# Two repeated waits ahead of the last matmul of each half of the up products, on one core

## The chip, the cores and the metric

The kernel runs on one core of one Trainium2 chip. The metric is the device time of one execution in microseconds, and the number to predict is the median of several executions. The core has five engines with an instruction stream each: TensorE (PE, with its weight loads shown apart as PEld), VectorE (DVE), ScalarE (ACT), GpSimd (POOL) and SyncE (SP). [...]

## What is computed

Two branches read the same 2048 x 512 input and a sigmoid gate per row mixes them:

```python
def reference(A_x, A_wq, A_wk, A_wv, A_wo, A_beta, B_x, B_w_gate, B_w_up, B_w_down, gate_w):
    x = A_x
    g = _sigmoid((x * gate_w).sum(-1, keepdims=True))
    a = _A_ref(x, A_wq, A_wk, A_wv, A_wo, A_beta)      # attention in 4 segments, 32 heads of 16
    b = _B_ref(x, B_w_gate, B_w_up, B_w_down)          # (gelu(x wg) * (x wu)) wd, inner width 1792
    return g * a + (1 - g) * b
```

The attention works on four segments of 512 rows. Inside a segment each head has causal softmax attention; across segments it reads a running memory M (16 x 16 per head) and its normaliser z, and both are updated with the segment's keys and values. A sigmoid of beta mixes the two per head.

## The kernel before

**Work and tiles.** Everything is done per segment s = 0 to 3. `project` (L504) makes K, Q and V with 128x128 weights and 512 moving columns; `memory` (L567) reads and updates M and z; `attend` (L683) computes scores for all heads in fills of the 2048-column PSUM tile psX (`fill`, L633: matmuls at L645, exponentials on ACT at L661, the causal mask on POOL at L667) and then the products with V (L698), turned and normalised on DVE (L557, L709, L710); `glu_gate` and `glu_up` (L800, L818) make 14 gate and 14 up products per segment; `outputs` (L827) makes four row blocks with the down weights (L837) and the attention's output weights (L854), joins them on DVE (L858) and stores them by DMA (L863).

**The up products.** `dense` (L483) builds one product of four accumulating matmuls as two tasks of two matmuls each: U3_5a and U3_5b are the first and second half of the up product of tile 5 in segment 3. There are 4 x 14 = 56 up products, so 112 such tasks. All dense products share line L487, and a 512-column PSUM bank (psD) of four takes each of them.

**Order and waits.** The order of all tasks is one long list, `ORDER` (L1015), found by a planner that is not part of the kernel. A word names a task, and behind the colon the PSUM bank or buffer that it begins, or the engine that it runs on (a for ACT, d for DVE) where an eviction may run on either. `Emitter.plan` (L176) derives what each instruction depends on, `finalize` (L205) turns that into waits on counting semaphores and leaves out every wait that an earlier one of the same engine has already covered, and `emit` (L237) writes the waits (L241) ahead of the instruction.

**The two paths and the last branch.** The kernel holds a fast program, and behind it a general one that is only run when the fast one's softmax sums are out of range. A flag is computed on the chip (L728 to L738), every engine loads it into a register (L742), and then its fast stream ends with a compare-and-branch (L961) over the general program to a label `done`. The general program is long: on TensorE the fast stream has 2767 entries (a matmul entry becomes a weight load and a matmul) and the general one 3801. Early in each stream stands a hint (L951) that names that branch as one likely to be taken; `HINT` (L27) says behind how many entries (6 on TensorE).

```python
        em.emit(eng, slice(p.start, p.start + HINT[eng]))
        ahead = e.mark_branch_hint_location()
...
        e.br_eq(regs[eng], GOOD, on_true=done, on_false=general).branch_hint(ahead)
        with nc.body(general, valid_engines=[e.engine]):
            em.emit(eng, q)
...
        nc.switch_bb(done)
```

At the end all engines meet in a barrier (the lines at L971), which SyncE joins once the last output has landed (L992).

Of the kernel before, what the change touches and what calls it, by code (L numbers as in the profile page):

```python
# [160 lines left out]
class Emitter:  # L161


    def __init__(self, nc, engmap):
        self.engmap = engmap
        self.cnt = {e: nc.alloc_semaphore(f"cnt_{e}") for e in (PE, ACT, DVE, POOL)}
        self.dma_val = {}
        self.res = {}
        self.streams = {e: [] for e in ENGINES}
        self.order = []  # L170

# [65 lines left out]
    def emit(self, eng, part):  # L237
        e = self.engmap[eng]
        for spec in self.streams[eng][part]:
            for sem, val in spec.waits:  # L240
                e.wait_ge(sem, val)  # L241
            ins = spec.fn(e)
# [11 lines left out]
def _build(es, nc, A_x, A_wq, A_wk, A_wv, A_wo, A_beta, B_w_gate, B_w_up, B_w_down, gate_w, out):  # L254
# [30 lines left out]
    ident = sb("ident", [P, P])  # L285
# [14 lines left out]
    gr1 = sb("gr1", [P, 16], F32)  # L300
# [639 lines left out]
    for turn_ in (order, program(True)[0].in_turn()):  # L940
# [4 lines left out]
        parts.append({e: slice(began[e], len(em.streams[e])) for e in ENGINES})  # L945
    em.finalize()
# [74 lines left out]
V0_0a:0 Qev0_1:a V0_3a:1 st0_0A:0 V0_1a:2 V0_0b exp0_0A vones0 causal Vev0_0:d V0_1b V0_3b V0_2a:3 Vev0_1:d Vev0_3:d
ld_wg1 st0_0B:0 V0_2b exp0_0B phka0_2 Vev0_2:a vsh0_00 phkc0_0 G0_6a:2 vsh0_01 G0_6b msk0_0A Gev0_6:d G0_2a:0 G0_1a:1
st0_0C:0 G0_1b G0_3a:3 Gev0_1:d exp0_0C G0_0a:2 G0_0b G0_2b Gev0_0:d st0_0D:0 vsh0_20 exp0_0D vsh0_21 msk0_0B G0_3b
betab Gev0_3:d ld_wu1 Q1_3a:2 ld_wo00 msk0_0D Q1_3b G1_6a:1 G1_6b Qev1_3:d Gev0_2:d bexp ld_wo10 Gev1_6:d st0_0E:0
Q1_2a:3 K1_1a:2 V1_3a:0 Q1_2b K1_1b exp0_0E Qev1_2:d msk0_0C st0_1A:0 V1_0a:1 msk0_0E V1_0b V1_3b Kev1_1:a Vev1_0:d gq
pv0_0:23 exp0_1A phkb0_2 ld_wo30 Vev1_3:d st0_1B:0 exp0_1B V1_1a:1 Q1_1a:0 V1_1b Q1_1b tp0_d01:1 Qev1_1:a K1_2a:3
phkc0_2 ld_x2_1 st0_1C:0 Vev1_1:d G0_4a:1 exp0_1C G0_4b tp0_d00:2 K1_0a:2 K1_0b K1_3a:0 Gev0_4:d Kev1_0:a st0_1D:0
exp0_1D ktr0_1 kpada1_1 G0_5a:1 pvp0_00 G1_1a:2 G0_5b K1_3b pvp0_01 Gev0_5:a K1_2b st0_2A:0 ld_wo11 ktr0_3 exp0_2A
G1_1b G1_7a:1 ktr0_2 Kev1_3:d Kev1_2:d G0_10a:0 ld_x2_2 Gev1_1:d G1_7b G0_8a:3 msk0_1A gph G0_10b gd0_10 kpada1_0
G0_8b ld_wo01 G1_13a:2 gd1_7 G1_13b msk0_1D msk0_1C G0_9a:0 kpada1_2 phqa1_2 gd1_13 G0_9b ld_wu0 G0_13a:1 G0_13b  # L1030
G0_7a:2 gd0_8 msk0_1B gd0_9 ot0_0 pv0_1:03 gd0_13 st0_2B:0 G1_9a:1 gelu0 G0_7b tp0_d10:1 G1_9b G0_12a:0 gd0_7
tp0_d11:0 G1_8a:3 G0_12b G0_11a:2 pvp0_10 G1_8b pvp0_11 gd1_9 G0_11b gd0_12 Q1_0a:1 kpadb1_1 gd1_8 Q1_0b U0_3a:3
Qev1_0:d gd0_11 U0_3b G1_5a:0 G1_5b ktr0_0 ld_wd0 h0_3 ld_wo21 phka1_0 kpada1_3 U0_9a:1 U0_11a:3 U0_11b exp0_2B U0_9b
st0_2C:0 ot0_1 mz0:2 phkb1_0 msk0_2B h0_9 U0_5a:1 h0_11 ld_x2_0 exp0_2C U0_5b msk0_2C phka1_2 ld_gw U0_8a:3 Gev1_5:a
ld_xg0 gs0 st0_2D:0 kpadb1_2 U0_8b exp0_2D mzacc0 U0_6a:2 U0_6b h0_5 U0_1a:0 h0_8 U0_4a:3 ld_xg1 gs1 h0_6 st0_2E:0
msk0_2A U0_1b U0_4b U0_7a:2 phkc1_0 h0_1 exp0_2E U0_13a:1 U0_7b st0_3A:0 ld_xg2 ld_xg3 h0_4 G1_0a:0 phkb1_2 G1_0b
ld_xg4 msk0_2D U0_13b h0_7 gs2 exp0_3A msk0_2E ld_xg5 pv0_2:32 Gev1_0:a h0_13 st0_3B:0 U0_0a:0 tp0_d20:1 U0_10a:1
V1_2a:3 V1_2b U0_10b exp0_3B gs3 tp0_d21:0 phqa1_0 st0_3C:0 U0_2a:2 h0_10 U0_0b gs4 msk0_3A h0_0 U0_2b h0_2 G1_2a:1
kpadb1_0 Vev1_2:a G1_2b exp0_3C ld_x2_3 kpadb1_3 st0_3D:0 msk0_3B G1_3a:0 mzm0 K2_1a:2 ld_xg6 K2_1b G1_4a:3 exp0_3D
msk0_3C msk0_3D Gev1_2:d Kev2_1:a G1_3b st1_0A:0 U0_12a:1 exp1_0A ld_xg7 pvp0_21 G1_4b Gev1_3:d gs5 U0_12b pvp0_20  # L1040
h0_12 pv0_3:20 zq0 st1_0B:0 phqb1_2 out0_1_0:1 out0_1_1 ld_wd1 exp1_0B tp0_d30:2 phkc1_2 K2_3a:2 ld_x3_3 tp0_d31:0 gs6
out0_1_2 gs7 ktr1_0 st1_0D:0 K2_3b Q2_3a:0 ktr1_2 vsh1_00 out0_1_3 Gev1_4:a Kev2_3:d exp1_0D Q2_3b gz0 K2_2a:3 msk1_0B
ot0_2 ktr1_1 Qev2_3:a st1_0E:0 gr0 vsh1_01 phqc1_2 V2_3a:2 K2_0a:0 V2_3b K2_2b Vev2_3:d pvp0_30 exp1_0E out0_1_4
st1_0C:0 K2_0b go0 Kev2_2:a ld_wo20 ktr1_3 phqb1_0 Kev2_0:d out0_3_0:3 vsh1_21 msk1_0A G1_11a:2 pvp0_31 out0_0_0:0
ot0_3 out0_0_1 out0_0_2 wev0_1:d exp1_0C out0_0_3 out0_0_4 wo0_1_0:1 vsh1_20 out0_3_1 G1_11b wev0_0:d out0_3_2
# [81 lines left out]
```

## Time and profile before

| what | value |
|---|---|
| median of 3 runs | 267.12 us (267.05, 267.12, 267.35) |
| profiled execution, its own time | 268.07 us |
| its span, first to last instruction | 266.3 us |
| mean granted TensorE clock | 0.997 |
| TensorE matmuls busy | 254.0 us, 95% of the span |
| DVE, ACT, POOL busy | 214.5, 209.6, 96.6 us |
| last arithmetic (the copy of the flag, L738) ends | 261.0 us |

The span leaves 1.8 us of the profiled execution's own time outside, and that execution took 0.95 us longer than the median. Engines named with a q (PEldq, SPq) are their sequencers: waits, branches and DMA issues, which are not counted as busy. A group's "idle before" is time in which its engine stood still just ahead of it, with what ended that. DMA queues are named by number; those of the kind "instruction" bring the engines' own code.

### The profile page before, as it was taken

The page shows a single profiled execution, that of the slowest core. Times are in us where ns is not written, and L with a number is a line of the kernel's source. Part 1 is how long each engine was busy: PE and PEld are TensorE (multiplying, and loading weights), DVE is VectorE, ACT ScalarE, POOL GpSimd, SP SyncE. Part 2 cuts the span into 40 slices and gives each one's busy share as a digit, 9 for nine tenths or more (in the row PEclk, how much of TensorE's full clock was granted, in tenths as well). Part 3 has the DMA queues.
Part 4 walks back from the last instruction along what each step waited for, and adds up shares of the span by engine and source line. Part 5 has one row for each costly group of instructions (what it writes and reads, how often), then busy time and mean ns, then how long its engine had stood idle before and what let it go on. Part 6 is the DMA issues. An engine that isn't in the chain of part 4 may idle for free.

```text
span 266.3 us, 6561 instructions
## 1 busy us (share of the span) xinstructions
PE 254.0 (95%) x2729; PEld 112.4 (42%) x2766; DVE 214.5 (81%) x421; ACT 209.6 (79%) x174; POOL 96.6 (36%) x159
## 2 busy tenths in 40 slices
PE   7999999999999999999999999999999999999991
PEld 4634434444344444444434344334444443434450
DVE  0676776689999797999798989998988986959872
ACT  2578999989899999999988879568889976577420
POOL 6024332065551526160452644433407217263400
PEclk9999999999999999999999999999999999999998
DMA  6897179802547203002021001000110000000011
GB/s 205 237 177 234 39 108 192 245 23 62 158 62 100 61 20 109 12 0 63 0 64 42 20 2 62 2 21 2 43 35 7 0 2 21 21 22 1 22 39 47
DMA packets 26624, 17.19 MB, mean 65 GB/s; under 512 B 14302, under 2 KB 26078, under 8 KB 26590
## 3 DMA queue, kind: packets, MB, share of 16 engines
q1 hardware_dynamic: 26014, 16.27, 25.3%
q10 hardware_dynamic: 576, 0.46, 0.6%
q8 instruction: 22, 0.36, 0.6%
q14 instruction: 12, 0.10, 0.1%
HBM read 10.36 MB, written 2.10 MB: 47 GB/s over the span
## 4 chain that ended last, share of the span: by engine, by line
PE 93%; issue 2%; DMA 2%; DVE 1%; SPq 0%
PE psD L487 51%; PE psD L837 18%; PE psX L645 9%; PE psD L698 6%; PE psD L854 5%; DMA pt<-in_A_x_dram 2%; PE psD L582 1%; PE psD L515 1%; PE psX L600 0%; PE psD L509 0%; DVE ost L858 0%; SPq L357 0%; PE psD L588 0%; PE psX L908 0%; DVE kD L526 0%
## 5 line engine op out<-in xcount | busy, mean ns | idle before, releaser
L661 ACT ACTIVATE pt<-psX 128x2048 bf16<-128x2048 f32 x72 | 135.1, 1877 | 28.6 <-PE psX L645 27.4
L667 POOL TENSOR_TENSOR pt<-pt,ctri 128x256 bf16<-128x256 bf16 x128 | 91.2, 719 | 151.8 <-ACT pt L661 147.3
L487 PE MATMUL psD<-xT,wu 128*128 128x512 bf16 x214 | 54.1, 380 | 1.4 <-issue 1.3
L837 PE MATMUL psD<-wd,gb 128*128 128x512 bf16 x217 | 54.1, 380 | 0.9 <-issue 0.8
L487 PE MATMUL psD<-xT,wg 128*128 128x512 bf16 x217 | 54.1, 380 | 0.9 <-issue 0.8
L824 DVE TENSOR_TENSOR gb<-psD,gb 128x512 bf16<-128x512 f32 x56 | 37.3, 684 | 8.6 <-PE psD L487 8.3
L837 PEld LDWEIGHTS psD<-wd,gb 128*128 128x128 bf16 x224 | 20.5, 98 | 26.1 <-issue 2.8
L487 PEld LDWEIGHTS psD<-xT,wu 128*128 128x128 bf16 x224 | 20.3, 98 | 26.1 <-issue 2.8
L487 PEld LDWEIGHTS psD<-xT,wg 128*128 128x128 bf16 x224 | 20.1, 98 | 26.4 <-issue 3.2
L557 DVE STREAM_TRANSPOSE tT<-psD 128x512 f32<-128x512 f32 x35 | 24.1, 703 | 7.7 <-PE psD L698 5.8
L645 PE MATMUL psX<-qT,kD 32*128 32x192 bf16 (+7 forms) x512 | 28.5, 287 | 0.0
L645 PEld LDWEIGHTS psX<-qT,kD 32*128 32x128 bf16 x512 | 8.2, 92 | 25.2 <-ACT pt L661 20.9
L698 PE MATMUL psD<-pt,vnat 64*17 64x128 bf16 (+7 forms) x512 | 18.8, 283 | 0.0
L698 PE MATMUL psD<-pt,vsh 64*17 64x128 bf16 (+7 forms) x512 | 18.3, 283 | 0.0
L710 DVE SCALAR_TENSOR_TENSOR ob<-tT,gq,rcall 128x256 bf16<-128x256 f32 x32 | 16.6, 517 | 1.1
L487 PE MATMUL psD<-wv,xT 128*128 128x512 bf16 x61 | 16.8, 380 | 0.4 <-issue 0.3
L487 PE MATMUL psD<-xT,wq 128*128 128x512 bf16 x59 | 16.2, 379 | 0.7 <-issue 0.5
L480 DVE CAST gb<-psD 128x512 bf16<-128x512 f32 x19 | 12.9, 686 | 3.9 <-PE psD L487 3.9
L854 PE MATMUL psD<-wo,oT 128*128 128x512 bf16 (+1 forms) x69 | 15.5, 354 | 0.5 <-issue 0.5
L698 PEld LDWEIGHTS psD<-pt,vnat 64*17 64x17 bf16 x512 | 11.6, 86 | 8.9 <-POOL pt L667 4.2
L815 ACT ACTIVATE gb<-psD 128x512 bf16<-128x512 f32 x28 | 14.8, 603 | 0.6 <-PE psD L487 0.5
L842 ACT ACTIVATE wds<-psD,omgt 128x512 f32<-128x512 f32 x8 | 5.5, 686 | 12.1 <-PE psD L837 7.4
(99 smaller groups left out, 275.8 us busy)
## 6 DMA issues: line engine op xcount, KB each, us to landing
xg<-in_A_x_dram SPq DMA_DIRECT2D x16, 128.0 KB, 2.2
out_dram<-ost SPq DMA_DIRECT2D x15, 128.0 KB, 1.7
wg<-in_B_w_gate_dram SPq DMA_DIRECT2D x2, 896.0 KB, 6.8
wu<-in_B_w_up_dram SPq DMA_DIRECT2D x2, 896.0 KB, 5.9
wd<-in_B_w_down_dram SPq DMA_DIRECT2D x2, 896.0 KB, 6.7
vsh<-vnat SPq DMA_DIRECT2D x16, 68.0 KB, 2.1
wq<-in_A_wq_dram SPq DMA_DIRECT2D x2, 256.0 KB, 5.3
wv<-in_A_wv_dram SPq DMA_DIRECT2D x1, 512.0 KB, 3.9
```

The costliest lines, as they stand in the source:

```text
L480: (DVE, 0.60, [I(lambda e: e.tensor_copy(dst, src()), [bk(sl), *reads], writes)]),
L487: one(f"{name}{'abcd'[h // 2]}", PE, 2 * T_MM, [I(lambda e, i=i: e.matmul(BK[sl.i][:, :], lhs(i), rhs(i), start=(i == 0), stop=(i == n - 1 ...
L557: one(f"tp{name}", DVE, 0.605, [I(lambda e, ts=ts, bank=bank: e.transpose(tT[ts.i][:, :], bank()), [key], [("tT", ts)])])
L645: ins.append(I(lambda e, c=c, kb=kb, ncol=ncol, c0=c0, g=g: e.matmul(XALL[:, g * 512 + c0:g * 512 + c0 + ncol], kD[b][quad(g), c, kb, :], ...
L661: one(f"exp{s}_{name}", ACT, 2048 * 0.000833 + 0.05, [I(lambda e: e.activation(pt[slot][:, :, :], xin, ACTF.Exp, scale=ATT_SCALE), [("X", ...
L667: ins.append(I(lambda e, mv=mv: e.tensor_tensor(mv, mv, cm, ALU.mult), [("pt", slot), ("causal",)], [("pt", slot)]))
L698: ins.append(I(lambda e, kb=kb, slot=slot, c0=c0, n=n, g=g, c=c, r0=r0, sl=banks[j], va=va: e.matmul(BK[sl.i][32 * c:32 * c + 17, 64 * kb: ...
L710: I(lambda e, ts=ts, t=t, j=j, dst=dst, r=r: e.scalar_tensor_tensor(out=dst, in0=t_rows(ts, 16), scalar=gq[:, 2 * t + j:2 * t + j + 1], in ...
L815: one(f"gd{s}_{ft}", ACT, 0.485, [I(lambda e, gi=gi, f=f, sl=sl: e.activation(gb[gi][:, f, :], BK[sl.i][:, :], ACTF.Gelu_apprx_tanh), [bk( ...
L824: one(f"h{s}_{ft}", DVE, 0.605, [I(lambda e, sl=sl, gi=gi, f=f: e.tensor_tensor(gb[gi][:, f, :], BK[sl.i][:, :], gb[gi][:, f, :], ALU.mult ...
L837: mm.append(I(lambda e, fb=fb, gi=gi, f=f, q=q, sl=sl: e.matmul(BK[sl.i][:, :], gb[gi][:, f, q], wd[:, fb, :], start=(fb == 0), stop=(fb = ...
L854: one(f"wo{s}_{qt}_{ci}", PE, 4 * T_MM / len(parts), [I(lambda e, kb=kb, q=q, so=so, c=c: e.matmul(BK[so.i][:, c], oT[:, kb, q], wo[:, kb, ...
```

## The change

Each instruction gets a field `again`. For every task of the fast order whose name begins with U, on TensorE, the last instruction (the second of its two matmuls) gets `again = 2`. While writing the stream, `emit` remembers the last wait that it wrote for an engine and, ahead of an instruction with `again`, writes that same wait (same semaphore, same value) twice more. As the engine has met it already, it holds nothing up by its value. The general program does not get the repeats.

```diff
@@ class Instr
-    __slots__ = ("fn", "reads", "writes", "dma_sem", "waits", "deps", "inc")
+    __slots__ = ("fn", "reads", "writes", "dma_sem", "waits", "deps", "inc", "again")
...
+        self.again = 0
@@ class Emitter
+        self.met = {}
...
             for sem, val in spec.waits:
                 e.wait_ge(sem, val)
+                self.met[eng] = sem, val
+            for _ in range(spec.again):
+                e.wait_ge(*self.met[eng])
             ins = spec.fn(e)
@@ _build
+    for t, eng, instrs in order:
+        if t.name[0] == "U":
+            instrs[-1].again = 2
     em.finalize()
```

`ORDER` is replaced as a whole by a newly planned one of the same 1203 words. The two begin and end so:

```diff
-ld_x0_0 wake0:0 ld_x0_1 ld_wk0 ident wake1 ld_wk1 xtr0_00 ld_x0_2 xtr0_01 ld_x0_3 ld_wk2 ld_wq0 xev0_00:a xev0_01:a
-xtr0_03 xtr0_02 ld_wq1 xev0_02:d K0_k0:0132 K0_k1 xtr0_10 xev0_03:d ld_wv ld_beta ld_wg0 xtr0_11 ld_x1_2 xev0_10:a
...
-wo3_2_0:2 wev3_3:a wo3_2_1:3 oev3_2_0 wo3_3_0:0 wo3_3_1:1 oev3_2_1 dma13_0 oev3_3_0 oev3_3_1 oksum:2 dma14_1 dma15_0
-flag dma15_1 reg_pe reg_act reg_dve reg_pool reg_sp
+ld_x0_0 causal1 wake0:0 ident ld_x0_1 ld_wk0 wake1 ld_wk1 xtr0_00 ld_x0_2 xtr0_01 ld_x0_3 ld_wk2 xtr0_03 xev0_00:a
+xev0_01:d xev0_03:d ld_wq0 xtr0_02 ld_wq1 xev0_02:d K0_k0:1032 ld_wv K0_k1 xtr0_11 xtr0_10 ld_beta ld_wg0 xtr0_12
...
+oev3_2_0 wo3_2_1:0 wo3_3_0:2 oev3_2_1 wev3_3:a wo3_3_1:3 oksum:1 oev3_3_0 oev3_3_1 flag dma14_1 dma15_0 dma15_1 reg_pe
+reg_act reg_dve reg_pool reg_sp
```

Of the 524 TensorE tasks, 266 keep their place among TensorE's tasks and none moves by more than 7 places. Of the 100 evictions that may run on either engine, DVE has 57 before and 55 after, ACT 43 and 45.

More of the change, by code (lines that the diff above doesn't have):

```diff
@@ L1021 @@
[L1021 to L1045, printed above, removed]
@@ new lines @@
+K0_2b phka0_0 Kev0_3:d Q0_0a:0 Kev0_2:a Q0_2a:1 ld_x1_1 Q0_2b Q0_0b consts Q0_1a:2 ld_x1_0 phkb0_0 ld_x1_3 kpadb0_0
+kpada0_0 kpada0_2 kpadb0_3 causal kpadb0_2 Qev0_0:a Q0_3a:3 Qev0_2:a kpadb0_1 Q0_3b Q0_1b V0_3a:1 kpada0_1 V0_0a:0
+Qev0_3:d Qev0_1:a kpada0_3 st0_0A:0 exp0_0A vones0 V0_1a:2 V0_1b V0_0b V0_2a:3 Vev0_1:d V0_3b st0_0B:0 G0_6a:2
+Vev0_3:d V0_2b Vev0_0:d G0_6b G0_2a:0 exp0_0B ld_wg1 G0_1a:1 vsh0_00 phka0_2 Vev0_2:a st0_0C:0 exp0_0C vsh0_01 G0_1b
+msk0_0C msk0_0B Gev0_6:d G0_2b G0_0a:3 vsh0_21 phkc0_0 G0_0b G0_3a:2 vsh0_20 st0_0D:0 G0_3b Gev0_1:d betab Gev0_2:d
@@ new lines @@
+G1_6a:0 ld_wu1 Q1_3a:1 Gev0_3:d exp0_0D G1_6b Gev1_6:a msk0_0D Q1_3b Gev0_0:d st0_0E:0 ld_wo00 Qev1_3:d Q1_2a:2
+K1_1a:0 ld_wo10 exp0_0E K1_1b Q1_2b bexp V1_3a:1 Kev1_1:d st0_1A:0 V1_0a:0 ld_wo30 Qev1_2:d msk0_0A V1_0b V1_3b
+msk0_0E Vev1_3:d pv0_0:23 Vev1_0:d exp0_1A st0_1B:0 V1_1a:1 V1_1b phkb0_2 tp0_d01:2 ld_x2_1 exp0_1B Q1_1a:0 tp0_d00:0
+msk0_1A gq K1_2a:3 Q1_1b Qev1_1:d st0_1C:0 K1_0a:2 Vev1_1:a exp0_1C K1_0b K1_3a:0 G0_4a:1 ktr0_1 G0_4b st0_1D:0
+exp0_1D K1_3b phkc0_2 Kev1_0:d pvp0_01 ld_wo11 Kev1_3:a Gev0_4:d G1_1a:2 kpadb1_1 ktr0_3 K1_2b G0_5a:1 msk0_1D G0_5b
@@ new lines @@
+st0_2A:0 Kev1_2:d exp0_2A Gev0_5:d ktr0_2 G0_8a:3 G1_1b msk0_1B G0_10a:0 G0_10b gd0_10 ld_x2_2 G1_7a:1 Gev1_1:d
+kpadb1_3 G1_13a:2 ld_wo01 kpadb1_0 G1_7b ld_wu0 msk0_1C G1_13b gd1_7 ktr0_0 G0_8b gd0_8 G0_9a:0 kpadb1_2 G0_9b
+G0_13a:1 G0_13b phqa1_2 kpada1_2 gd0_9 pvp0_00 st0_2B:0 gd1_13 pv0_1:03 gd0_13 gelu0 G0_7a:2 G1_9a:1 tp0_d10:1 G0_7b
+gd0_7 tp0_d11:0 G1_9b G0_12a:3 G1_8a:0 G0_12b G1_8b G0_11a:2 G0_11b gd1_9 Q1_0a:1 gph gd1_8 kpada1_0 kpada1_3 ot0_0
+gd0_12 ld_wd0 Q1_0b gd0_11 pvp0_10 U0_3a:0 U0_9a:3 G1_5a:2 msk0_2A phka1_2 Qev1_0:d U0_3b G1_5b ld_wo21 pvp0_11
@@ new lines @@
+ld_x2_0 exp0_2B U0_11a:1 h0_3 U0_11b U0_9b phka1_0 msk0_2B Gev1_5:d ld_gw h0_9 st0_2C:0 mz0:2 U0_8a:3 U0_5a:0 phkb1_0
+ld_xg0 h0_11 U0_5b gs0 exp0_2C st0_2D:0 kpada1_1 U0_8b mzacc0 U0_6a:2 U0_6b ld_xg1 U0_1a:1 U0_1b ld_xg2 exp0_2D
+st0_2E:0 exp0_2E gs1 h0_8 h0_6 U0_4a:3 msk0_2C msk0_2D ot0_1 h0_5 U0_4b h0_1 ld_xg3 h0_4 gs2 U0_7a:2 U0_7b h0_7
+G1_0a:1 phqb1_2 msk0_2E st0_3A:0 exp0_3A gs3 U0_13a:0 ld_xg4 ld_xg5 U0_13b h0_13 G1_0b pv0_2:32 Gev1_0:a ld_x2_3
+tp0_d20:1 st0_3B:0 U0_10a:1 U0_10b V1_2a:3 msk0_3A V1_2b tp0_d21:2 U0_0a:0 exp0_3B h0_10 st0_3C:0 U0_2a:2 exp0_3C
@@ new lines @@
+G1_2a:1 U0_0b phqa1_0 U0_2b pvp0_20 msk0_3C phkc1_0 h0_0 Vev1_2:a G1_2b st0_3D:0 K2_1a:0 h0_2 exp0_3D msk0_3B K2_1b
+G1_3a:2 mzm0 G1_3b G1_4a:3 Gev1_2:a gs4 msk0_3D gs5 st1_0A:0 G1_4b exp1_0A phkb1_2 msk1_0A U0_12a:1 Gev1_3:d ld_xg6
+ld_xg7 U0_12b Kev2_1:d Gev1_4:d h0_12 pv0_3:20 st1_0B:0 tp0_d30:1 pvp0_30 ld_wd1 out0_1_0:1 ld_x3_3 pvp0_21 out0_1_1
+tp0_d31:2 out0_1_2 exp1_0B K2_3a:2 st1_0D:0 phqb1_0 phkc1_2 K2_3b out0_1_3 K2_2a:0 Q2_3a:3 gs6 exp1_0D K2_2b ktr1_0
+Kev2_3:a Q2_3b ktr1_1 Kev2_2:a vsh1_01 ot0_2 msk1_0B Qev2_3:a st1_0E:0 phqc1_2 ktr1_2 msk1_0D K2_0a:2 V2_3a:0 V2_3b
@@ new lines @@
+Vev2_3:d exp1_0E K2_0b out0_0_0:3 st1_0C:0 Kev2_0:a out0_0_1 pvp0_31 exp1_0C kpada2_3 vsh1_00 ld_wo20 out0_3_0:0 gs7
+G1_11a:2 gz0 gr0 out0_1_4 zq0 ot0_3 go0 gelu1 kpada2_2 wev0_1:d out0_3_1 phqc1_0 out0_0_2 G1_11b out0_3_2 ktr1_3
+gd1_11 out0_3_3 wo0_1_0:1 out0_0_3 kpadb2_3 kpada2_1 out0_0_4 vsh1_21 vsh1_20 msk1_0C phka2_0 out0_3_4 msk1_0E
+oev0_1_0 st1_1A:0 wev0_0:d exp1_1A wev0_3:d pv1_0:12 ld_x3_2 tp1_d00:0 mz1:30 st1_1B:0 tp1_d01:2 dma1_0 Q2_1a:1
+phka2_2 Q2_1b mzacc1 msk1_1A out0_2_0:2 wo0_0_0:3 exp1_1B phkb2_2 kpadb2_0 tp1_z:1 Qev2_1:d st1_1C:0 ld_x3_1 ld_x3_0
@@ new lines @@
+Gev2_5:a kpadb2_1 Gev2_6:d G2_0a:0 pvp1_11 G2_0b st1_2D:0 G2_9b kpadb2_2 wo0_2_0:1 Gev2_0:d G2_8a:0 Gev2_1:d exp1_2D
+chk0 G2_12a:3 gd2_9 G2_12b st1_2E:0 oev0_2_0 msk1_2D gd2_12 phkc2_0 G2_8b G2_13a:1 gs8 G2_13b U1_3a:2 ndp1_1 U1_0a:3
+ld_xg11 U1_0b h1_0 U1_3b gd2_8 h1_3 U1_8a:0 gelu2 U1_8b h1_8 U1_1a:3 U1_1b phqa2_2 U2_5a:2 gd2_13 U1_5a:0 U1_5b
+V2_0a:1 V2_0b h1_1 msk1_2C wo0_3_0:3 h1_5 Q2_0a:0 exp1_2E Vev2_0:a pvp1_10 kpada2_0 U2_5b oev0_3_0 zq1 st1_3A:0 ktr2_0
+msk1_2B msk1_2E h2_5 U1_7a:1 gs9 Q2_0b ot1_0 exp1_3A U1_7b pv1_2:23 Qev2_0:a dma2_0 st1_3B:0 h1_7 V2_1a:0 V2_1b
@@ new lines @@
+vsh2_01 V3_1b phqc2_0 h1_2 U2_3b exp2_0D h2_3 Vev3_1:a Q3_3a:0 st2_0E:0 ld_xg12 Q3_3b gs10 msk2_0C Qev3_3:d U2_7b
+msk2_0A U1_10a:3 exp2_0E U1_10b U1_6a:0 h2_7 h1_10 st2_1A:0 msk2_0D exp2_1A U1_6b pvp1_30 out1_0_0:1 msk2_0E pv2_0:32
+phqc2_2 h1_6 st2_1B:0 out1_0_1 U1_12a:0 ld_xg13 tp2_d00:2 ktr2_3 V3_3a:3 exp2_1B U1_12b tp2_d01:1 st2_1C:0 ot1_2
+K3_3a:2 V3_3b pvp2_01 out1_0_2 K3_3b msk2_1B out1_0_3 exp2_1C Kev3_3:a h1_12 st2_1D:0 Vev3_3:a out1_0_4 exp2_1D
+V3_2a:2 ot1_3 mz2:30 pvp2_00 wev1_0:a st2_2A:0 gs11 tp2_z:2 msk2_1C msk2_1A V3_2b wo1_0_0:1 ld_xg14 mzacc2 msk2_1D
@@ new lines @@
+exp2_3A wo1_2_0:1 msk2_2E ndp2_0 pv2_2:32 oev1_2_0 st2_3B:0 exp2_3B U2_11a:1 U2_8a:0 kpada3_1 U2_8b U2_11b tp2_d20:0
+tp2_d21:1 gs14 h2_8 G3_5a:3 st2_3C:0 U2_2a:2 h2_11 G3_3a:0 exp2_3C msk2_3B G3_3b G3_5b U2_2b Gev3_5:a st2_3D:0 phqa3_0
+kpadb3_2 exp2_3D msk2_3C wo1_3_0:1 phqb3_0 dma5_0 Gev3_3:d U2_12a:3 oev1_3_0 U2_4a:0 U2_12b st3_0A:0 U2_4b h2_2
+msk2_3A exp3_0A msk2_3D h2_12 G3_0a:2 G3_0b pv2_3:31 st3_0B:0 ot2_0 h2_4 Gev3_0:a pvp2_20 U2_9a:2 exp3_0B msk3_0B
+tp2_d31:0 pvp2_21 U2_9b V3_0a:0 vsh3_20 V3_0b h2_9 G3_1a:1 st3_0C:0 exp3_0C Vev3_0:d G3_1b G3_4a:2 msk3_0C G3_4b
@@ new lines @@
+st3_1B:0 out2_0_0:3 out2_0_1 phqb3_2 ot2_3 h3_5 msk3_1A tp3_d00:1 out2_1_0:1 exp3_1B tp3_d01:2 U3_6a:2 st3_1C:0
+phqc3_2 pvp3_00 out2_1_1 out2_1_2 out2_1_3 mz3:0 exp3_1C st3_1D:0 out2_0_2 out2_1_4 mzm2 U3_6b exp3_1D msk3_1C tp3_z:0
+out2_2_0:0 st3_2A:0 out2_0_3 wev2_1:a wo2_1_0:1 nzp3 out2_2_1 exp3_2A nd3:0 pvp3_01 out2_2_2 h3_6 oev2_1_0 msk3_1D
+out2_0_4 tp3_m3:0 out2_2_3 wev2_0:a dma9_0 out2_2_4 tp3_m1:1 msk3_1B ndp3_3 tp3_m2:2 tp3_m0:0 pv3_1:32 st3_2B:0 ndp3_2
+tp3_d11:2 wo2_0_0:1 oev2_0_0 ndp3_0 out2_3_0:2 out2_3_1 exp3_2B wev2_2:a msk3_2A st3_2C:0 tp3_d10:0 dma8_0 U3_0a:1
@@ new lines @@
+U3_0b h3_0 exp3_2C out2_3_2 wo2_2_0:0 st3_2D:0 U3_1a:1 pvp3_11 msk3_2B exp3_2D U3_10a:3 out2_3_3 U3_1b msk3_2C
+st3_2E:0 oev2_2_0 exp3_2E U3_10b U3_7a:0 h3_1 h3_10 out2_3_4 U3_7b U3_4a:3 msk3_2D st3_3A:0 ndp3_1 U3_4b msk3_2E h3_7
+out3_0_0:1 wev2_3:d pvp3_10 exp3_3A pv3_2:20 h3_4 st3_3B:0 wo2_3_0:3 tp3_d21:2 out3_1_0:0 exp3_3B ot3_0 oev2_3_0
+out3_1_1 st3_3C:0 U3_9a:3 out3_0_1 exp3_3C chk2 tp3_d20:0 U3_9b h3_9 msk3_3B out3_1_2 st3_3D:0 exp3_3D out3_0_2
+pvp3_21 out3_1_3 dma10_0 msk3_3C out3_0_3 msk3_3A out3_0_4 dma11_0 msk3_3D pvp3_20 out3_2_0:2 out3_2_1 wev3_0:a ot3_2
```

76 lines of the change are left out of this document (23 added, 53 removed).

## The prediction

> **What bounds the kernel now.** I read the page first: how long TensorE is busy, and what the chain of work that ended last is made of.
>
> ```profile
> span 266.3 us, 6561 instructions
> ...
> PE 254.0 (95%) x2729; PEld 112.4 (42%) x2766; DVE 214.5 (81%) x421; ACT 209.6 (79%) x174; POOL 96.6 (36%) x159
> ...
> PE 93%; issue 2%; DMA 2%; DVE 1%; SPq 0%
> ```
>
> TensorE is the bound of the body: 93% of the chain is its matmuls, and no other engine is over 81% busy. A change to the body can win only what TensorE loses between matmuls. But the arithmetic does not run to the end of the span. The chain's last pieces, in order of time:
>
> ```profile
> 258.69 1.32 PE psD L854 x12
> 260.01 0.03 issue
> 260.04 0.92 DVE ost L858 x2
> 260.96 0.05 DVE flag L738
> ```
>
> The copy of the flag ends at 261.0, and 266.3 - 261.0 = 5.3 us follow in which no engine computes. So the next thing to read is the sequencers there: the line of the last branch (L961), then the barrier's line (L971) and SyncE's waits. Columns: engine, operation, count, duration in ns (least/median/most), start of the first and the last.
>
> ```profile
> L961 POOLq COMPARE_BRANCH  x1: 65/65/65, 261.6 to 261.6; - x1
> L961 PEldq COMPARE_BRANCH  x1: 4322/4322/4322, 261.6 to 261.6; - x1
> L961 SPq COMPARE_BRANCH  x1: 83/83/83, 261.6 to 261.6; - x1
> L961 DVEq COMPARE_BRANCH  x1: 84/84/84, 261.8 to 261.8; - x1
> L961 ACTq COMPARE_BRANCH  x1: 68/68/68, 261.9 to 261.9; - x1
> ```
>
> ```profile
> L971 SPq DRAIN  x1: 13/13/13, 262.9 to 262.9; - x1
> L971 PEldq DRAIN  x1: 63/63/63, 266.0 to 266.0; - x1
> ```
>
> ```profile
> SPq L971 <- PEq L971: 3.3, 1, 3.3
> ...
> SPq L992 <- DMA out_dram<-ost: 0.9, 1, 0.9
> ```
>
> Four engines take the same kind of branch in 65 to 84 ns; TensorE needs 4322 ns. SyncE, which first waits 0.9 us for the last output to land, is at the barrier at 262.9 and then waits 3.3 us for TensorE alone. **The end of the span is TensorE's branch.**
>
> Why it is slow shows in the DMA queues of kind "instruction". The last column but one is MB; the first two rows are those of the whole span (the page), the next is of 236 to 248 us, the last two of 262 to 266.4 us. The same view of 248 to 262.5 us has no instruction row at all.
>
> ```profile
> q8 instruction: 22, 0.36, 0.6%
> q14 instruction: 12, 0.10, 0.1%
> ```
>
> ```profile
> q8 instruction: 2, 0.03, 1.2%
> ```
>
> ```profile
> q8 instruction: 1, 0.02, 2.7%
> q14 instruction: 4, 0.03, 2.4%
> ```
>
> Narrowing the windows to 0.1 us puts q8's packets at 236.91, 247.36 and, inside the branch, 262.55. Now the instructions between them (matmuls and loads, the counts behind x in the first two columns after the length; first row from the first q8 packet after the start to that at 247.36, then the two last intervals):
>
> ```profile
> 15.34:247.36 232.02, 227.21 (x2522) 97.64 (x2554) 197.27 (x377) 198.56 (x159) 90.36 (x129) 1.00 0.24 57
> ```
>
> ```profile
> 236.91:247.36 10.45, 10.29 (x128) 4.33 (x127) 8.57 (x17) 8.06 (x6) 4.76 (x8) 1.00 0.05 16
> 247.36:261.60 14.24, 12.86 (x126) 6.80 (x126) 11.45 (x27) 3.96 (x5) 1.83 (x3) 1.00 0.09 29
> ```
>
> q8 is TensorE's code. It moves 0.36 MB / 22 = 16.4 KB a time, once per 2 x 2554 / 20 = 255 matmuls and loads and some waits, so per 256 instructions of 64 bytes: a block. The last block was fetched at 247.36, the branch is the 253rd or 254th instruction after that (126 + 126, the load of the flag), and only then comes the next fetch, 0.95 us into the branch. **Reading A:** a fetch begins about 1 us after TensorE enters a block; the branch is among the first instructions of a new one, and the fetch of its target, which the hint asks for on entering the branch's own block, has had no head start. **Reading B:** the fetch of 247.36 should have been that of the target, and the hint fails on TensorE. For A: four hinted branches elsewhere hit, and those engines had eight of their twelve q14 fetches ahead of the end and, as the row has it, four just after their branches, as an engine has that goes on into code already there. For B: nothing here shows a hint at work on TensorE.
>
> **The change part by part.** *The repeats.* 112 halves get two waits each. One wait rides on an instruction and a second becomes an instruction of its own: in the lists of before (L205), 38 TensorE entries of the fast path have two waits and one has three, and the profile has 39 semaphore instructions of line L241 on TensorE.
>
> ```profile
> L241 PEldq EVENT_SEMAPHORE  x39: 51/51/51, 1.6 to 239.4; - x39
> ```
>
> The matmul entries that get the repeats have no wait of their own (their inputs and weights were waited for by the first of the half). So each half adds one 51 ns semaphore instruction, 112 in all, and one wait on a weight load. The sequencer pays 112 x 0.051 = 5.7 us; TensorE pays only what isn't hidden. The cover is the first matmul of the half. Of it and its load:
>
> ```profile
> 256.96 1.73 PE psD L837 x8
> ```
>
> ```profile
> L487 PEld LDWEIGHTS psD<-xT,wu 128*128 128x128 bf16 x224 | 20.3, 98 | 26.1 <-issue 2.8
> ```
>
> Dense matmuls follow each other every 1.73 / 8 = 0.216 us; load and semaphore take 98 + 51 = 149 ns, so 67 ns are left. If the cover were gone, 51 ns each would show. That a met wait costs nothing on a running stream is seen at U0_3a, whose first load carries two waits by the lists. Its semaphore instruction ran at 48.8, and TensorE's timeline from 46.03 on has no idle time at it:
>
> ```profile
> 49.70 1.03 PE L487 MATMUL psD<-xT,wq 128*128 128x512 bf16 x4
> 50.56 1.03 PE L487 MATMUL psD<-xT,wu 128*128 128x512 bf16 x4
> 51.42 1.03 PE L487 MATMUL psD<-xT,wg 128*128 128x512 bf16 x4
> ```
>
> The products start 0.86 us apart, four matmuls of 0.216. Bounds: 0 and +5.7 us, and no gain, as a wait speeds nothing up; I take 0, the value of this row. It is also the nearest: same line, same tile, a second wait.
>
> *The branch.* It moves 112 places along, plus or minus the few two-wait instructions that the new order makes more or fewer. Under A it then stands some 112 places into its block. How much earlier is that block entered?
>
> ```profile
> 251.60:261.60 10.00, 8.82 (x49) 4.70 (x48) 7.94 (x19) 2.06 (x3) 0.00 (x0) 1.00 0.12 41
> ```
>
> 97 instructions run in the last 10.0 us, so 112 take a little more. The fetch needs 4.3 us at most, so it is done 5 us ahead, and the branch takes about 0.08 us as on the other four. What is late next is SyncE's arrival at 262.9, behind the landing of the last output: 0.9 us after TensorE's new arrival at about 261.9. From there the barrier's end costs what it does now. Gain by the barrier rows: 266.05 (start and length of TensorE's drain) - 262.88 = 3.2 us, as SyncE's waiting row says too (3.3). Bounds: 0 (B) and 3.3. The first 0.95 us of the stall are lag and the packet itself takes up to 1.9 (2.7% of 16 engines over 4.4 us); an unprofiled execution may fetch faster, up to the 0.95 us that lies between 268.07 and 267.12, so at least 2.2 under A.
>
> [...]
>
> *The order.* 266 of 524 TensorE tasks keep their place, the rest shift by up to 7; two evictions go from DVE to ACT, so neither stream's branch moves by more than a few places. No TensorE row but at the start waits for a DMA, so moved DMA issues cost nothing unless one comes late. What an order can win or lose are TensorE's waits for evictions:
>
> ```profile
> PEld psD L487 <- ACT gb L815: 1.2, 4, 0.4
> PEld psD L487 <- DVE tT L557: 0.9, 4, 0.3
> PEld psD L837 <- DVE tT L557: 0.9, 4, 0.4
> ```
>
> These sum to 3.0 us in 12 waits, which is the most that I see to win, and as many again the most to lose. With moves this small I take 0, and 0.8 us (three such waits of 0.25) to either side.
>
> **The sum.** In the profiled execution: 266.3 + 0 - 3.2 + 0 = 263.1 us of span, 1.8 around it: 264.9. The median of before is 0.95 under its profiled execution, so 267.12 - 3.2 = 263.9, **264.0 us** with the rounding. Its own range: 263.2 (order -0.8) to 265.7 (stall 1.0 shorter without a profile, order +0.8).
>
> **The rivals.**
> *The branch still stalls* (reading B, or another engine's branch that the new order puts at the start of a block). For it: the fetch of 247.36 may have been for the wrong block. Against: four hits. Time 267.1, by the order's 0.8 from 266.3 to 267.9. [...]
> *The repeats show.* Place: between the two matmuls of each up half. If the waiting load can't slip under the running matmul or the sequencer isn't ahead, each costs up to 51 ns: 5.7 - 3.2 = +2.5, 269.6 us. It decides from 3.2 / 112 = 28 ns each. Against: 67 ns of room, and U0_3a. For: that row has one such place, not 112.
>
> **How the numbers follow.** Forecast 0.70, branch still stalls 0.22, repeats show 0.08. The second case falls about a quarter each to faster and slower and half to no change. A measurement of this kernel tells 0.2% (0.5 us) from no change. Faster: 0.69 + 0.05 = 0.74. Same: 0.01 + 0.10 = 0.11. Slower: 0.07 + 0.08 = 0.15. The range goes from 263.2 up to 267.4, so that it holds the forecast's own (0.64 of it) and over half of the second case: 0.64 + 0.03 + 0.13 = 0.80.
>
> **What would show each step.** L961 on PEldq near 0.08 us, and no SPq L971 row behind PEq; one q8 fetch between 248 and 256 us and none inside the branch; about 151 semaphore instructions of 51 ns on TensorE and up products still 0.86 us apart. Wrong would be: the branch at some 4 us again (B), gaps of tens of ns at the second and fourth matmul of L487 with wu, or TensorE's last matmul off its 260.4 us by more than 0.8.

## The result, and the profile after

| what | before | after |
|---|---|---|
| median, 16 executions each | 267.09 us (266.36 to 268.60) | 264.92 us (264.47 to 266.87) |
| ratio of the means (267.16 and 265.36 us) | | 0.9933, 95% interval 0.9912 to 0.9954 |
| profiled execution, its own time | 268.07 us | 266.08 us |
| its span | 266.3 us | 264.3 us |

The change makes the kernel 2.2 us faster in the median and 1.8 us in the mean. The ratios given are not those of the medians (here 0.9919) and differ from them by up to 0.0014. An execution over 1.5% slower than the fastest of its kernel is left out of them; this concerns one, of `after_again`. First the page of the changed kernel: span, busy time, chain.

```profile
span 264.3 us, 6669 instructions
...
PE 254.2 (96%) x2729; PEld 112.7 (43%) x2766; DVE 215.7 (82%) x419; ACT 210.7 (80%) x176; POOL 100.6 (38%) x159
...
PE 95%; issue 2%; DVE 1%
```

TensorE's arithmetic is what it was, 254.2 us against 254.0; the span is 2.0 us shorter. The new lines push the line numbers on: the branch (L961) is L969 now, the barrier (L971) L979, SyncE's wait for the last output (L992) L1000; dense products are L492, the memory's matmuls (L582) L587.

The last branch in the changed kernel (columns as for L961):

```profile
L969 POOLq COMPARE_BRANCH  x1: 65/65/65, 262.8 to 262.8; - x1
L969 PEldq COMPARE_BRANCH  x1: 390/390/390, 262.9 to 262.9; - x1
L969 SPq COMPARE_BRANCH  x1: 83/83/83, 262.9 to 262.9; - x1
```

And SyncE's last waits in it (total us, times, longest):

```profile
SPq L1000 <- DMA out_dram<-ost: 0.9, 1, 0.9
...
SPq L979 <- PEq L979: 0.2, 1, 0.2
```

TensorE's branch fell from 4322 to 390 ns, and SyncE's wait for TensorE at the barrier from 3.3 to 0.2 us. That is a gain of 3.1 us. But the branch begins at 262.9, and it began at 261.6 before: in this execution the body is later by 1.25 us. Following TensorE task by task, the changed kernel is 0.28 us *early* at the first product with V in segment 1 (92.04 against 92.32 us), and 1.25 us late at the next one (109.53 against 108.28) and at every one from there to the end. So one place between them lost 1.53 us. TensorE's timeline there, first of the kernel before, then of the changed one (start, length, engine, line; in brackets the idle time ahead):

```profile
93.42 0.78 PE L582 MATMUL psD<-vnat,phkt 128*32 128x34 bf16 x64
94.04 0.40 PE L588 MATMUL psD<-phq,zq 128*8 128x512 bf16 x4
```

```profile
93.02 0.20 PE L703 MATMUL psD<-pt,vnat 64*17 64x64 bf16 x4
93.14 0.59 PE L587 MATMUL psD<-vnat,phkt 128*32 128x34 bf16 x46
95.22 0.30 PE L587 MATMUL psD<-vnat,phkt 128*32 128x34 bf16 x18 [1.49 <-issue]
```

The 64 small matmuls that update the memory in segment 1 (the task mz1) ran in one go; now TensorE stops after the 46th for 1.49 us, "issue": it waits for nothing that the profile shows. The queue of TensorE's code (q8; packets, MB, share) shows what for. Of the changed kernel, the view of 84 to 92.3 us has no q8 row; that of 92.3 to 94 us has:

```profile
q8 instruction: 1, 0.02, 5.0%
```

The packet starts at 92.39 and takes 1.36 us, to 93.75, when TensorE has just stopped. The next matmul runs 1.47 us after that. In the profile of the kernel before the same fetch began at 88.27. pv1_0 and mz1 are 128 instructions each, weight loads and matmuls together, and run in 1.1 and 0.8 us: a whole block in about 1.9 us, where a fetch from first packet to first instruction took 2.8 (92.39 to 95.22). Here the fetch came only with the burst, and TensorE ran dry.

**Where the blocks lie.** In `after` the stop falls ahead of the 47th matmul of mz1, in the kernel `order_alone` below ahead of the 61st. Counted along TensorE's stream, both are the same place. Behind the packet of 92.39 q8 has 15 more up to the branch, the last at 253.28: as reading A has it, one for each block from mz1's to the branch's. With blocks of 256 (an estimate from the prediction's rows: 16.4 KB a packet, one per 255 matmuls and loads and some waits), the last border is then 14 x 256 = 3584 instructions further on. The branch stands 3589 instructions behind that place before, so 5 places into its block, and 3696 in the changed kernel, 112 places into it. These places, and those given for the runs below, are good to one.

### The profile page after: what moved, and what is told of

Same layout as the page of the kernel before. It is cut to its first block, busy times and chain, and to the rows that moved or that the text cites. A ratio compares the mean times of both kernels' runs of the same rounds, so it can differ in the third digit from the quotient of the medians.

```text
span 264.3 us, 6669 instructions
## 1 busy us (share of the span) xinstructions
PE 254.2 (96%) x2729; PEld 112.7 (43%) x2766; DVE 215.7 (82%) x419; ACT 210.7 (80%) x176; POOL 100.6 (38%) x159
## 4 chain that ended last, share of the span: by engine, by line
PE 95%; issue 2%; DVE 1%
PE psD L492 52%; PE psD L842 19%; PE psX L650 9%; PE psD L703 7%; PE psD L859 5%; PE psX L404 1%; PE psD L514 1%; PE psD L587 1%; PE psD L520 1%; PE psX L913 1%; DVE gb L829 0%; PE psX L605 0%; DVE ost L863 0%; PE psD L593 0%; DVE mzacc L619 0%
## 5 line engine op out<-in xcount | busy, mean ns | idle before, releaser
L672 POOL TENSOR_TENSOR pt<-pt,ctri 128x256 bf16<-128x256 bf16 x128 | 95.1, 750 | 149.1 <-ACT pt L666 144.7
L492 PE MATMUL psD<-xT,wu 128*128 128x512 bf16 x216 | 55.3, 380 | 1.2 <-issue 1.1
L492 PE MATMUL psD<-xT,wg 128*128 128x512 bf16 x215 | 53.6, 379 | 1.1 <-issue 1.0
L492 PEld LDWEIGHTS psD<-xT,wg 128*128 128x128 bf16 x224 | 20.4, 98 | 26.3 <-issue 3.4
L492 PEld LDWEIGHTS psD<-xT,wu 128*128 128x128 bf16 x224 | 20.1, 98 | 25.9 <-issue 2.6
L847 ACT ACTIVATE wds<-psD,omgt 128x512 f32<-128x512 f32 x10 | 6.9, 686 | 13.0 <-PE psD L842 7.9
L492 PE MATMUL psD<-wv,xT 128*128 128x512 bf16 x61 | 16.1, 380 | 0.5 <-issue 0.5
L492 PE MATMUL psD<-xT,wq 128*128 128x512 bf16 x60 | 16.1, 379 | 0.5 <-DVE gb L829 0.2
```

Of the source, the lines that this page charges most:

```text
L492: one(f"{name}{'abcd'[h // 2]}", PE, 2 * T_MM, [I(lambda e, i=i: e.matmul(BK[sl.i][:, :], lhs(i), rhs(i), start=(i == 0), stop=(i == n - 1 ...
L672: ins.append(I(lambda e, mv=mv: e.tensor_tensor(mv, mv, cm, ALU.mult), [("pt", slot), ("causal",)], [("pt", slot)]))
```

## The experiments

Each run's time stands beside that of the kernel before on the same chip: 267.07 us (25 executions) for `order_alone`, `repeats_old_order`, `late112_new_order` and `late28_old_order`; 267.32 (11) for `early_border`, `late28_again`, `late28_no_hint` and `late08_old_order`; 267.12 (14) for `after_again`, `early_border_again`, `early_border_old_order` and `late16_old_order`. The diffs show the lines that matter; "old order" means that of the kernel before, with the fields `again` and `met` added as in the change.

**`order_alone`: the new order without the repeats.**

```diff
-    for t, eng, instrs in order:
-        if t.name[0] == "U":
-            instrs[-1].again = 2
```

> The changed kernel without its repeats: the new order alone. Its stream has five two-wait instructions fewer than the old one, so the last branch stands 5 places ahead of where it stood before. Theory 1 (a branch needs its block to have been entered some 4 us ahead; before, it was the first instruction of a block): it now is among the last of the block that was entered about 250 instructions earlier, and takes under 0.5 us; the stall of 1.5 us that the changed kernel has in the memory matmuls at 93 us goes or shrinks, as the block borders move by 28 places there; time 263.3 to 264.3. Rival (the hint fails near a block's end, or the repeats are what cures the branch): the branch takes about 4.3 us and the time is 266.5 to 267.5.

Measured: 268.71 us, ratio 1.0068 (1.0036 to 1.0101), slower than before. The branch and mz1:

```profile
L966 PEldq COMPARE_BRANCH  x1: 4332/4332/4332, 263.3 to 263.3; - x1
```

```profile
93.93 0.74 PE L587 MATMUL psD<-vnat,phkt 128*32 128x34 bf16 x60
95.78 0.20 PE L587 MATMUL psD<-vnat,phkt 128*32 128x34 bf16 x4 [1.11 <-issue]
```

The expectation failed: I had put the block's border five instructions too late. By the border that mz1 shows, the branch of this kernel (3584 instructions behind it) is the first of a new block, or the second, and it stalls in full. The new order alone gains nothing.

**`repeats_old_order`: the repeats in the order of before.**

```diff
+    for t, eng, instrs in order:
+        if t.name[0] == "U":
+            instrs[-1].again = 2
```

> The old order with the repeats, the branch 112 places further. Both theories have the branch under 0.5 us. Theory 1 (the 1.5 us stall at 93 us comes from code that arrives late, set by where a block border falls): the border falls 28 places earlier in the burst than in the old order, the fetch starts when the waits ahead of the burst are met (about 90.1 + 0.9), so code is there at about 93.5 to 94: a stall of 0 to 0.5 us, time 263.9 to 264.5. Rival 2 (the repeats cost time in the body): the up products come over 0.86 us apart, time 265 or more, with no single stall. Rival 3 (the new order costs the 1.3 us): time 263.9 or less.

Measured: 265.74 us, ratio 0.9955 (0.9935 to 0.9975). The branch took 380 ns, 117 places into its block. But mz1 stopped here too, for longer than expected:

```profile
94.73 0.30 PE L587 MATMUL psD<-vnat,phkt 128*32 128x34 bf16 x18 [1.02 <-issue]
```

So the stop doesn't need the new order. Nor does it need repeats ahead of it, as `late28_again` below shows.

**`late112_new_order`: the new order, all 112 semaphore instructions in segments 2 and 3, two on each half.**

```diff
-    for t, eng, instrs in order:
-        if t.name[0] == "U":
-            instrs[-1].again = 2
+    ups = [instrs[-1] for t, eng, instrs in order if t.name[:2] in ("U2", "U3")]
+    for i in ups[0:]:
+        i.again = 4
```

> The new order with four repeats on each of the 56 halves of segments 2 and 3 (two semaphore instructions each, 112 in all): the branch stands where the changed kernel has it, but nothing is moved ahead of the burst at 93 us. Theory 1: branch under 0.5 us, and the 1.5 us stall in the memory matmuls at 93 us is gone or under 0.5 us: 263.3 to 264.3, faster than the changed kernel by 0.7 to 1.5. Rival 2 (the repeats cost time): 102 ns of semaphores in 56 places against 67 ns of room costs 56 x 0.035 = 2 us or more, 266 or more.

Measured: 265.86 us, ratio 0.9945 (0.992 to 0.997); branch 380 ns; mz1 stops for 1.20 us although no repeat stands ahead of it, which was not expected. From the second group of products with V in segment 1 to the last one it keeps step with the kernel before to 0.01 us (1.53 us later at each group), with 102 ns of met waits in each half of segments 2 and 3: here the waits cost nothing.

**`late28_old_order` and `late28_again`: the old order, repeats on the 28 halves of segment 3 only.**

```diff
+    ups = [instrs[-1] for t, eng, instrs in order if t.name[:2] == "U3"]
+    for i in ups[0:]:
+        i.again = 2
```

> The old order with repeats on the 28 halves of segment 3 only: 28 semaphore instructions, all behind 200 us, so the body up to there is that of before and the branch moves by 28 places. Theory 1: the block is entered 28 instructions ahead of the branch, at about 258 to 259 us, the fetch starts about 1 us later and code is there at 262 to 263.5: the branch takes 0.5 to 2 us, a part of the 4.3. Rival (a hint hits or misses as a whole): either about 4.3 us or about 0.1 to 0.4 us, with no fetch of TensorE's code between 257 and 261 us in the first case.

> The old order with the repeats on segment 3 alone once more, now timed. Theory (only the branch is mended and no block border ahead of segment 3 moves, so nothing is lost in mz1): 264.0 to 264.6 us, ratio to the kernel before 0.988 to 0.991, faster than the changed kernel by about 0.5 us. Rival (the one look was a lucky run): 264.9 to 265.5, as the changed kernel.

Measured: one execution took 264.44 us, branch 473 ns at 33 places, no stop in mz1, fetch for it at 87.89. The fetch for the branch came at 256.22, earlier than expected and 1.9 us before TensorE ran the first weight load of the branch's block (258.14): it did not wait for TensorE's arithmetic to reach that block. Timed, the same kernel had 264.93 us (264.25 to 266.30), ratio 0.9901 (0.9867 to 0.9934), the median 0.3 us over what was expected, and in that profile a stop of 0.91 us, with the fetch at 92.73. **The same program stops in one execution and not in another.** So the stop in mz1 isn't a fixed price, and its absence in the one profile of before was no proof that before is free of it.

**`early_border` and `early_border_again`: the new order, as many repeats, but placed so that the border falls 28 instructions earlier ahead of mz1.** The branch keeps its place.

```diff
-        if t.name[0] == "U":
-            instrs[-1].again = 2
+        if t.name[0] == "U":
+            instrs[-1].again = {"U0": 4, "U1": 2, "U2": 2, "U3": 0}[t.name[:2]]
```

> The new order and again 112 repeated waits, so the branch stands at the same place of the stream as in the changed kernel (112 places into its block), but the repeats of segment 3 are left out and segment 0 has twice as many: every block border up to the end of segment 2 falls 28 instructions (some 2.5 us) earlier in the program, or less as segment 3 goes on. Theory (TensorE's code came late for the burst of pv1_0 and mz1): the block that mz1 runs into is fetched by 88, not at 92.39, the 1.49 us of idle time ahead of L587's x18 in segment 1 are gone or under 0.3, the branch stays at 0.4 us, span 262.6 to 263.2, time 263.2 to 264.2. Rival (the idle time in mz1 belongs to the new order itself, a wait that the profile doesn't name): it stays at 1.2 to 1.6 us, time 264.5 to 265.5.

> The new order with the repeats of segment 3 moved to segment 0, once more. Theory: no idle time ahead of L587 in segment 1 in any execution, so no run above 265.4 us and a median of 264.5 to 264.9. Rival (the late fetch was absent by luck in the first 6 runs): a part of the runs at 265.6 to 266.9 again.

Measured: 264.82 us (264.43 to 265.16), ratio 0.9901 (0.9869 to 0.9933), and again 264.79 (264.30 to 265.15), ratio 0.9909 (0.9882 to 0.9936). The fetch came at 84.54 us, and 83.97 again, and mz1 is whole in both profiles. Of the first:

```profile
93.24 0.79 PE L587 MATMUL psD<-vnat,phkt 128*32 128x34 bf16 x64
```

Here the place of the border decides: with the order, the number of repeats and the branch as in the changed kernel, the stop is gone from both profiles, and of 12 executions none is above 265.16. The first expectation was for 264.2 at most; the median missed that by 0.6.

**`after_again`: the changed kernel itself, beside the last two.**

> The changed kernel unaltered, beside the two next on one chip. Theory (its block border, 30 instructions ahead of a wait of pv1_0, lets the fetch for mz1 come late in some executions only): times in two groups, some of 264.4 to 265.0 and some of 265.6 to 266.9, median 264.6 to 266.0. Rival (the idle time in mz1 is there in every execution): one group around 266.

Measured: 265.21 us, ratio 0.9928 (0.9903 to 0.9953): four executions at 264.40 to 264.81 and four at 265.61 to 265.97. A ninth took 268.56; the median of all nine is 265.61. With the 16 above, 13 of 25 lie at 264.40 to 264.98 and 11 at 265.61 to 266.87. This time the profiled execution (264.68 us) was of the lower group. Its mz1, its body from 92 to 260 us (length, then busy time and instructions of PE, PEld, DVE, ACT, POOL, then clock, DMA share and GB/s), and below it that of the kernel before:

```profile
93.27 0.83 PE L587 MATMUL psD<-vnat,phkt 128*32 128x34 bf16 x64
```

```profile
92.00:109.00 17.00, 16.68 (x280) 7.63 (x286) 14.26 (x26) 16.14 (x16) 5.44 (x8) 1.00 0.27 72
109.00:260.00 151.00, 147.72 (x1632) 64.62 (x1632) 129.66 (x243) 117.88 (x92) 59.05 (x81) 1.00 0.08 22
```

```profile
92.00:109.00 17.00, 16.68 (x267) 7.48 (x276) 15.04 (x29) 15.88 (x15) 5.79 (x7) 1.00 0.23 61
109.00:260.00 151.00, 147.72 (x1639) 64.44 (x1639) 130.62 (x246) 116.20 (x89) 56.33 (x82) 1.00 0.08 22
```

Without the stop, TensorE is busy 16.68 and 147.72 us in both kernels. The two profiles of one program show when the fetch is late. TensorE's semaphore instructions in 88.4 to 89.2 and in 91 to 92.35 us, first of `after` (the stop), then of `after_again`:

```profile
L243 PEldq EVENT_SEMAPHORE  x2: 51/51/51, 88.8 to 88.9; - x2
...
L243 PEldq EVENT_SEMAPHORE  x3: 51/51/51, 91.4 to 91.9; - x3
```

```profile
L243 PEldq EVENT_SEMAPHORE  x2: 51/51/51, 88.9 to 89.0; - x2
...
L243 PEldq EVENT_SEMAPHORE  x3: 51/51/51, 91.6 to 91.8; - x3
```

The last one at 88.9 or 89.0 stands at the border; the one at 91.4 or 91.6, 30 places into the new block, is pv1_0's wait for its inputs. In `after_again` the fetch starts at 89.99, some 0.95 us behind the first of these; in `after` at 92.39, some 0.95 us behind the second. It reads as if a fetch that hasn't begun when the sequencer stops at a wait is put off until that wait is met. That isn't shown: in the four profiles with the border of before that stopped, the fetch came 1.1 to 1.2 us behind the second semaphore instruction of the new block and not behind its first. Other transfers weren't in the way: in `after` this core's DMA engines move nothing between 87.0 and 92.2 us. Nor do the waits explain it: `before` and `late08_old_order` run the same instructions up to there, with the semaphore instructions ahead of the burst at 87.26 and 90.09 us in both, but the fetch began at 88.27 in the one and at 92.25, with a stop, in the other. Why it had begun in the one execution and not in the other stays open.

**`early_border_old_order`: the same cure in the order of before.**

```diff
+            instrs[-1].again = {"U0": 6, "U1": 2, "U2": 0, "U3": 0}[t.name[:2]]
```

> The old order with 6 repeats on each second half of segment 0, 2 on those of segment 1 and none on the others: 112 semaphore instructions as before, the branch 117 places into its block, the border for mz1 44 instructions ahead of the next one that waits. Theory (order and repeats cost nothing by themselves, borders are all): no idle time in mz1, branch 0.4 us, median within 0.3 us of the same made with the new order, so 264.3 to 265.2. Rival (the new order wins or loses between engines what the block borders hide): 0.5 us or more between the two.

Measured: 264.71 us (264.20 to 265.20), ratio 0.9901 (0.9874 to 0.9928), beside 264.79 of `early_border_again` on the same chip, and mz1 is whole. The new order is worth nothing that these runs could tell.

**`late28_no_hint`: `late28_old_order` without TensorE's hint.**

```diff
-        ahead = e.mark_branch_hint_location()
+        ahead = e.mark_branch_hint_location() if eng != PE else None
...
-        e.br_eq(regs[eng], GOOD, on_true=done, on_false=general).branch_hint(ahead)
+        b = e.br_eq(regs[eng], GOOD, on_true=done, on_false=general)
+        if ahead is not None:
+            b.branch_hint(ahead)
```

> The old order, the repeats on segment 3 alone, and the branch hint taken out of TensorE's program (the other engines keep theirs); the branch stands 33 places into its block less the one of the hint instruction. Theory (the hint has the target fetched while the block is run): without it the branch takes 3.5 to 4.5 us again, no fetch of TensorE's code between 246 us and the branch, SyncE waits some 3 us at the barrier, span 266. Rival (the place in the block alone is what counts, the fetch would come anyway): 0.4 to 0.6 us and a span of 262.7.

Measured: 267.31 us in one execution. Branch, then the q8 rows of 246 to 261.6 and of 261.6 to 265 us:

```profile
L969 PEldq COMPARE_BRANCH  x1: 3537/3537/3537, 261.7 to 261.7; - x1
```

```profile
q8 instruction: 1, 0.02, 0.4%
```

```profile
q8 instruction: 1, 0.02, 2.2%
```

The stall is back, 3537 ns against 473 with the hint (`late28_old_order`), one place apart: here the hint does the work, and reading B falls. But one detail was not expected. There is a fetch ahead of the branch, at 256.63, as with the hint (256.22). Without the hint it can't have been the target's, as the target's comes at 262.68, 1.0 us into the branch. So a fetch ahead of the branch came without the hint too, and it reads as if the hint changes what it brings (not shown): without the hint q8 has one packet more in the whole span (24 against 23).

**`late08_old_order` and `late16_old_order`: repeats on the first 8, or 16, halves of segment 3, for a branch 13 or 21 places into its block.**

```diff
+    ups = [instrs[-1] for t, eng, instrs in order if t.name[:2] == "U3"]
+    for i in ups[:8]:
+        i.again = 2
```

> The old order and the repeats on the first 8 second halves of segment 3 only, so the branch stands 13 places into its block (5 in the kernel before, 33 with 28 repeats). Theory (the fetch begins about 1 us after the sequencer enters the block, which runs up to 30 instructions ahead of the engine): fetch at 258 to 259 us, branch 0.4 to 0.8 us. Rival (the fetch is held up while the sequencer stands at a waiting instruction, here the load of the last matmul of all, until about 259.7): fetch at 260.4 to 261, branch 1.5 to 2.5 us.

> The old order with repeats on the first 16 second halves of segment 3: the branch stands 21 places into its block (at 13 it took 4322 ns, at 33 it took 473). Theory (the fetch begins 1 us after the sequencer enters the block unless it then stands at a wait): the border lies in the 32 loads and matmuls of L859 that run without a pause, so fetch at 257.5 to 260 us and branch 0.4 to 2.5 us. Rival (32 instructions of the block must be passed first): fetch only behind the branch's start, branch 4322 ns.

Measured, one execution each: 268.70 and 265.54 us, with mz1 stopping for 0.57 and 0.84 us. The branch at 13 places, then at 21:

```profile
L969 PEldq COMPARE_BRANCH  x1: 4322/4322/4322, 262.3 to 262.3; - x1
```

```profile
L969 PEldq COMPARE_BRANCH  x1: 478/478/478, 262.3 to 262.3; - x1
```

At 21 places the fetch began at 257.49 and the branch took 478 ns, as expected. At 13 both expectations failed: no fetch until 263.23, though TensorE ran the block's first weight load at 260.31. It began 1.0 us after the load of the flag into the register (261.74 to 262.23) had ended, as in the kernel before (261.54 and 262.55). That fits a fetch held back by the waits at the end of the stream, but by that of the flag and not the one I had named; it is not shown. Between 13 and 21 places the branch goes from 4322 to 478 ns, with no step between seen.

## Why the prediction was right, and where it was off

**What bounds the kernel: right.** The end was TensorE's branch. With the branch short, SyncE's wait for TensorE is 0.2 us and the span ends behind the landing of the last output.

**Reading A: right in kind.** At 0, 5 and 13 places into its block the branch took 4322 to 4332 ns; at 21 and 33 places 473 to 478; at 112 and 117 places 380 to 390. The gain at the barrier was 3.1 us against the 3.2 predicted. The branch's own time was off: 0.39 us and not the 0.08 of the other engines; SyncE still waits 0.2 us for TensorE, where I had no wait. Of the signs I had named, "one q8 fetch between 248 and 256" came (253.28), but `late28_no_hint` has such a fetch (256.63) and stalls (3537 ns), so by itself it tells nothing.

**The repeats at 0: right for their own cost.** One more semaphore instruction per half, 112 in all, and the up products keep their 0.86 us. In the changed kernel:

```profile
L246 PEldq EVENT_SEMAPHORE  x112: 51/51/51, 49.3 to 245.3; - x112
```

```profile
49.34 1.03 PE L492 MATMUL psD<-xT,wq 128*128 128x512 bf16 x4
50.20 1.03 PE L492 MATMUL psD<-xT,wu 128*128 128x512 bf16 x4
51.06 0.59 PE L492 MATMUL psD<-xT,wg 128*128 128x512 bf16 x2
```

I had counted on them to move the branch within its block, and left out that they shift the code against the other borders as well: 28 of them stand ahead of mz1, and its stop lies 14 matmuls earlier than in `order_alone`.

**The order at 0, give or take 0.8: right for the order, wrong for the body.** I expected gains and losses among waits for evictions, and there were none: from 109 to 260 us TensorE is busy for 147.72 us in both. But my last sign, TensorE's last matmul within 0.8 us of 260.4, came out at 261.7. The loss was mz1's 1.49 us, by code that came late: a term that I had at nothing, although I had just read the end of the kernel from the same queue. Whether the change makes this stop more frequent isn't shown: of six profiles with the border where it was before, to one instruction, four stopped, for 0.57 to 0.91 us.

Nearly all of the code came without such a loss: in the profile of the changed kernel q8 has 22 packets up to the branch, and TensorE's timeline from 12 to 262 us has one idle time of 0.2 us or more, this one; that of `after_again` has none.

**The sum: right for one execution, wrong for the median.** For an execution like the profiled one I had 263.1 us of span and 264.9 of time; `after_again`, without the stop, has 262.9 and 264.68, and the first profile of the changed kernel, with it, 264.3 and 266.08. The step that failed is the next one: "The median of before is 0.95 under its profiled execution, so" 264.0. I took the 0.95 us off the changed kernel too, as if both had it. They don't: 264.68 lies inside the lower group of the changed kernel (264.40 to 264.98), where before's executions scatter from 265.36 to 268.99.

In the medians the changed kernel gains 2.2 us, 1.9 in `after_again`, and the kernels whose mz1 is whole 2.3 to 2.5; the two profiles without a stop (268.07 and 264.68) differ by 3.4. An estimate from the means: the kernels whose mz1 is whole lie 2.6 to 2.7 us under the kernel before, less than the 3.1 us of the profiled branch alone, so that branch costs on average at least 0.4 us less than in its profile. I had kept such a case in the range ("stall 1.0 shorter without a profile"), and 264.92 fell there. That it came out at the upper edge of the lower group is luck: 9 of 16 executions were in that group, and in `after_again`, with four in each, the median fell between the two. How much of the scatter of before is its branch and how much its mz1 wasn't separated.

## What to carry to other kernels

TensorE's code came here in packets of 16.4 KB, one per 255 matmuls and loads and some waits, and where a border fell was part of the schedule: 112 semaphore instructions took the branch from 5 places into its block to 117, and from 4322 to 380 ns (`repeats_old_order`); 28 of them ahead of mz1 moved its stop by 14 matmuls. So when instructions are added, read the instruction queue's packets beside every "issue" gap, and above all ahead of bursts of short instructions (mz1's 64 matmuls run in 0.8 us). The gap was there in one execution of a kernel and not in another (1.49 us in `after`, none in `after_again`), so one profile without it proves nothing; the spread of the times tells more (264.40 to 264.98 and 265.61 to 266.87). And a difference between a profile's own time and the median belongs to something: subtract it from the new kernel only if you know that the change leaves it in place.

## What the runs showed of the hardware

- A late fetch of TensorE's code cost more than its packets. In the changed kernel they ended at 93.75, and the next matmul ran at 95.22 (1.47 us later). In the kernel before the target's packet ended at 264.43, and the branch at 265.92 (1.49). Over the eight stops in mz1 and the four stalled branches profiled, this gap is 1.28 to 1.62 us.
- Where TensorE's hinted branch did not stall, it took 380 to 478 ns; on the other four engines the branch took 65 to 84 in all profiles.
- Without the hint a fetch went out ahead of the branch too (256.63, `late28_no_hint`), and the branch took 3537 ns.
- Two programs, each profiled twice, stopped in mz1 once and not the other time: the changed kernel for 1.49 us, the one with 28 late repeats for 0.91. The order of the instructions did not fix when their code arrived.
- Four repeated waits in a half (two semaphore instructions, 102 ns, `late112_new_order`) left dense products of 0.86 us where they were.
